# Reordering the head of a fused transformer block: the first scaled activations, tile 2's transposes, and a split last K tile used as cover

## The chip, the core and the metric

The kernel runs on one core of a Trainium2 chip. The metric is the device time of one execution in microseconds (us). TensorE does the matmuls ("PE" in the profile; "PEld" is its weight load), VectorE is "DVE", ScalarE "ACT", GpSimdE "POOL", and SyncE ("SP") issues most transfers (71 of 79 in the trace of before). Where a start time has three decimals, or a "stall" or "gap" is given in nanoseconds, it is worked out from the recorded starts of consecutive instructions: the distance from one matmul's start to the next, less what that shape usually takes.

## The reference

A diffusion transformer block on 2 x 256 tokens of width 1152, with six modulation vectors from `silu(c) @ w_mod`:

```python
mod = (_silu(c) @ w_mod).reshape(B, 6, 1, D)
shift_a, scale_a, gate_a, shift_m, scale_m, gate_m = [mod[:, i] for i in range(6)]
h = _layernorm(x) * (1 + scale_a) + shift_a
qkv = (h @ wqkv).reshape(B, N, 3, H, Dh)
# attention over 2 heads of 576, then
x = x + gate_a * (a @ wo)
h2 = _layernorm(x) * (1 + scale_m) + shift_m
return x + gate_m * (_gelu(h2 @ w_fc1) @ w_fc2)
```

Only the stretch up to the first Q matmul is changed. It needs LN1 of four token tiles (0 and 1 are batch 0, 2 and 3 batch 1), the scale sums, K = h @ wk from a "scaled h" without the shift (a shift of all keys by one vector leaves the softmax as it is), then the shift, and Q.

## The kernel before

Instructions stand in units; a list scheduler orders ACT and DVE, and PE keeps program order. The code hangs an increment of its engine's semaphore on each instruction that is not a transfer; the trace of before records 1754 of them on TensorE's, for 1755 matmuls:

```python
for ins in u.instrs:
    for (k, v) in waits[ins.gidx]:
        ...                                        # wait_ge on other engines' or transfers' semaphores
    bi = ins.fn(eng_handle)
    if ins.dma_sem is not None:
        bi.then_inc(dma_sems[ins.dma_sem], 16)
    else:
        bi.then_inc(sems[e], 1)
```

The head. `warm` issues dummy matmuls, `xn_T(t)` transposes a tile's normalised rows, `sca` is the first four column groups of the scale sums, `hk(kt, b)` scales one k-tile of one batch, `k_first(kt)` multiplies it into K for batch 0 (eight 256-column matmuls):

```python
xn_T(0); warm(1, "d"); sca(3, 6); warm(2, "e"); sca(6, 9)
hk(0, 0); sc1a(0, KC); hk(1, 0)
# ... (copies of tile 0/1's transposes, hk(2,0) and hk(3,0) on ACT)
xn_T(3, 0, 8)
xn_T(2, 0, 8)
k_first(0)
xn_T(3, 8, 9); xn_T(2, 8, 9)
k_first(1)
# ...
k_pair(range(KC), 0, 1); k_pair(range(KC), 1, 1)      # batch 1, first four k-tiles
sc_ones(KC, KT)
for kt in range(KT):
    mod_kt(WSC, kt, 0, "scb_%d" % kt, (KC, KT))        # 45 two-column matmuls: second scale sums
sc1a(KC, KT)                                           # copy 1 + scale out of PSUM
for kt in range(KC, KT):
    for b in range(2):
        hk(kt, b)                                      # scaled h of k-tiles 4..8
k_pair(range(KC), 2, 1)                                # eight matmuls, cover for sc1a and hk(4, 0)
# k-tiles 4..8 (the "fifth k-tile" is kt = 4) ...
k_pair(range(5), 3, 1, bank=1)
#   shift rows: 36 matmuls with two output rows, packed four column tiles wide
copy_on("dve", SHR[0:98, :], ...)                      # evict them
k_pair(range(5, KT), 3, 1, bank=1)                     # eight matmuls, cover for that
#   nine transposes of the shift rows, copied to SHA; h = scaled h + SHA
proj(WK, 8, 17, HK, 0)                                 # last K tile: nine 512-column matmuls, cover for that
```

The output stage, which the change doesn't touch, ends with stores of 96 and 64 columns whose matmuls (36 each) come last.

Of the kernel before, what the change touches and what calls it, by code (L numbers as in the profile page):

```python
# [500 lines left out]
P = 128  # L501
NTOK = 512
D = 1152
KT = 9
# [5 lines left out]
CH = 384  # L510
NCH = 3
F0 = 8
KC = 4
# [3 lines left out]
def c_mm(n):  # L517
    return max(n / 2.4 + 2.5, 27.0)
# [26 lines left out]
def build_kernel(nc, x, c, wqkv, wo, w_mod, w_fc1, w_fc2, out):  # L545
    S = Sched()
# [4 lines left out]
    with (  # L551
# [11 lines left out]
        def ps32(bank, c0=0, n=512):  # L563
            return psum[:, bank * 512 + c0: bank * 512 + c0 + n]
# [30 lines left out]
        WK = wmat(O_B, D)  # L595
        WO = wmat(O_B, D)
        WSH = wmat(O_C, D)
# [12 lines left out]
        HK = sb(O_HK, 9216).rearrange("p (k t) -> p k t", k=KT)  # L610
        QK = sb(O_QK, 18432).rearrange("p (j t) -> p j t", j=18)
# [19 lines left out]
        IDENT = sb(misc(256), 256)  # L631
# [4 lines left out]
        ST = sb(misc(36), 36)  # L636
        SHA = sb(misc(72), 72, F32)
        SC1A = sb(misc(72), 72, F32)
# [32 lines left out]
        def dma(dst, src, nbytes, name, is_out=False, eng="sp", run=4096):  # L671
            eff = 0.95 if run >= 4096 else (1.0 if run >= 2304 else (1.08 if run >= 1536 else 1.14))
            return S.op(eng, 500.0 if eng == "sp" else 150.0, lambda e: e.dma_start(dst, src), reads=[src], writes=[dst],  # L673
                        name=name, dma_bytes=nbytes * eff, is_out=is_out)
# [10 lines left out]
        def copy_on(eng, dst, src, n, psum16, name):  # L685
            if eng == "act":
                act(c_act(n), lambda e: e.activation(out=dst, in_=src, func=ACTF.Copy), [src], [dst], name)  # L687
            else:
                dve(c_dve_psum16(n) if psum16 else c_dve_psum32(n), lambda e: e.tensor_copy(dst, src), [src], [dst], name)  # L689

        def mm(o, l, r, st, sp, **kw):
            S.instr(lambda e: e.matmul(o, lhsT=l, rhs=r, start=st, stop=sp, **kw), reads=[l, r], writes=[o])  # L692
# [82 lines left out]
        def xn_T(t, ka=0, kb=KT):  # L775
            b = t // 2
            S.unit("pe", (kb - ka) * c_mm(128), "xnT_%d_%d" % (t, ka))
            for kt in range(ka, kb):
                tr(xslot(b, kt)[:, (t % 2) * 128:(t % 2) * 128 + 128], XN[:, t, kt * 128:(kt + 1) * 128], IDENT)
# [5 lines left out]
        def warm(n, tag, behind=None):  # L785
            for i in range(n):
                S.unit("pe", 300.0, "warm_%s_%d" % (tag, i))
                mm(ps32(2), IDENT, Q4B, True, True)
                if behind:
                    S.instrs[-1].deps.update(j for j in S.instrs[:-1] if j.name == behind)  # L790

        def mod_kt(W, kt, col0, name, fs=(0, 9)):
            S.unit("pe", (fs[1] - fs[0]) * 27.0, name)
            for f in range(*fs):
                mm(ps32(7, col0 + f * 2, 2), W[:, kt, f * 128:(f + 1) * 128], ST[:, kt:18:9], False, kt == KT - 1, skip_group_check=True)

        def sc1a(ka, kb):
            m, o = ps32(7, 2 * ka, 2 * (kb - ka)), SC1A[:, 2 * ka:2 * kb]
            dve(180, lambda e: e.tensor_copy(o, m), [m], [o], "sc1a_%d" % ka)


        def hk(kt, b, eng="dve"):
            dst = HK[:, kt, b * 256:(b + 1) * 256]
            s1 = ps32(7, 0, 1) if kt == 0 and b == 0 else SC1A[:, kt * 2 + b:kt * 2 + b + 1]
            src = xslot(b, kt) if kt < KC else HX[:, kt, b * 256:(b + 1) * 256]
            if eng == "act":
                act(c_act(256, 1), lambda e: e.activation(out=dst, in_=src, func=ACTF.Copy, scale=s1), [src, s1], [dst], "hk_%d_%d" % (kt, b))
                return
            dve(345 if kt < KC else 285, lambda e: e.tensor_scalar(out=dst, in0=src, scalar1=s1, scalar2=None, op0=ALU.mult),
                [src, s1], [dst], "hk_%d_%d" % (kt, b))  # L810
# [8 lines left out]
        ev_rr = [0]  # L819

        def k_pair(kts, i, b, bank=None):
            S.unit("pe", 2 * len(kts) * c_mm(256), "k%d_%d_%d" % (b, i, kts[0]))
            bank = KB[b][i] if bank is None else bank
            if kts[0] == 0:
                for kt in kts:
                    for half in range(2):
                        k_mm((kt,), 2 * i + half, b, bank, half)
            else:
                for half in range(2):
                    k_mm(kts, 2 * i + half, b, bank, half)  # L830
            if kts[-1] == KT - 1:
                eng = "act" if ev_rr[0] % 2 == 0 else "dve"
                ev_rr[0] += 1
                copy_on(eng, QK[:, 9 + 2 * i:11 + 2 * i, b * 256:(b + 1) * 256], ps32(bank).rearrange("p (j t) -> p j t", j=2), 512, False,
                        "k_ev%d_%d" % (b, i))
# [5 lines left out]
        def sc_ones(ka, kb):  # L841
            S.unit("pe", 60.0, "ones_%d" % ka)
            mm(ps32(7, 2 * ka, 2 * (kb - ka)), IDENT, ONES[:, 2 * ka:2 * kb], True, True)
# [8 lines left out]
        xn_T(0)  # L852
        warm(1, "d")
        sca(3, 6)
        warm(2, "e")
        sca(6, 9)
        hk(0, 0)
        sc1a(0, KC)
# [3 lines left out]
        hk(2, 0, "act")  # L862
        hk(3, 0, "act")
        xn_T(3, 0, 8)
        xn_T(2, 0, 8)

        def k_first(kt):
            for i in range(4):
                k_pair((kt,), i, 0)

        k_first(0)
        xn_T(3, 8, 9)
        xn_T(2, 8, 9)
        k_first(1)
        xn_T_copy(1, 4, 8, "act")
        xn_T_copy(1, 8, 9, "act")
        for kt in range(2, KC):
# [2 lines left out]
            hk(kt, 1)  # L880
        k_pair(range(KC), 0, 1)
        k_pair(range(KC), 1, 1)
        sc_ones(KC, KT)
        for kt in range(KT):
            mod_kt(WSC, kt, 0, "scb_%d" % kt, (KC, KT))
        sc1a(KC, KT)
        for kt in range(KC, KT):
            for b in range(2):
                hk(kt, b)
        k_pair(range(KC), 2, 1)  # L890
        for kt in range(KT):
            dma(WQ[:, kt, :], wqkv_v[:, kt, 0:D], P * D * 2, "ld_wq%d" % kt, run=2304)
# [7 lines left out]
                k_pair((KT - 2, KT - 1), i, b)  # L900

        def qk_evac(j, bank):
            copy_on("act" if ev_rr[0] % 2 == 0 or j in (6, 8) else "dve", QK[:, j, :], ps32(bank), 512, False, "qk_ev%d" % j)
            ev_rr[0] += 1

        def proj(W, j, dst_j, H, bank):
            S.unit("pe", KT * c_mm(512), "qk_%d" % dst_j)
            for kt in range(KT):
                mm(ps32(bank), W[:, kt, j * 128:(j + 1) * 128], H[:, kt, :], kt == 0, kt == KT - 1)
            qk_evac(dst_j, bank)  # L910

        sh_split = ((0, 3), (3, 5), (5, 7), (7, 9))
        SHR = sb(O_P, 768)
        k_pair(range(5), 3, 1, bank=1)
        S.unit("pe", KT * c_mm(CH) + 100.0, "shr")
        for kt in range(KT):
            for j, (f0, f1) in enumerate(sh_split):
                mm(psum[32 * j:32 * j + 2, 1024:1024 + (f1 - f0) * 128], ST[:, kt:18:9], WSH[:, kt, f0 * 128:f1 * 128],
                   kt == 0, kt == KT - 1, tile_position=(0, 32 * j))
        copy_on("dve", SHR[0:98, :], psum[0:98, 1024:1024 + CH], CH, False, "shr_ev")  # L920
        k_pair(range(5, KT), 3, 1, bank=1)
        S.unit("pe", KT * 27.0, "shT")
        for j, (f0, f1) in enumerate(sh_split):
            for f in range(f0, f1):
                mm(ps32(2, f * 2, 2), SHR[0:98, (f - f0) * 128:(f - f0 + 1) * 128], IDENT[0:98, 32 * j:32 * j + 2], f == 0, f == KT - 1,
                   skip_group_check=True)
        dma(WV, wqkv_v[:, :, 2 * D:3 * D], D * D * 2, "ld_wv", run=2304)
        for k0 in range(0, KT, 3):
            dma(WMODR[:, k0:k0 + 3, :], wmod_v[:, k0:k0 + 3, 2 * D:4 * D], 3 * P * 2 * D * 2, "ld_modr%d" % k0)
        MT1 = ps32(2, 0, 18)  # L930
        dve(170, lambda e: e.tensor_copy(SHA, MT1), [MT1], [SHA], "sha")
        for kt in range(KT):
            for b in range(2):
# [5 lines left out]
                else:  # L939
                    dve(260, lambda e, src=src, dst=dst, s2=s2: e.tensor_scalar(out=dst, in0=src, scalar1=s2, scalar2=None, op0=ALU.add),  # L940
                        [src, s2], [dst], "hx_%d_%d" % (kt, b))
        proj(WK, 8, 17, HK, 0)
        dma(WO, wo_v, D * D * 2, "ld_wo", run=2304)


        S.first = {
            "dve": ["zq4b", "c_half", "c_silu", "bn_ln1_1_0", "bn_ln1_1_1", "bn_ln1_1_2", "aggr_ln1_1", "veps_ln1_1", "bn_ln1_2_0",
                    "xn_1", "bn_ln1_2_1", "xn_0", "bn_ln1_2_2", "aggr_ln1_2", "var_ln1_3", "veps_ln1_2", "xn_3", "xn_2", "hk_0_0", "sc1a_0", "hk_1_0",
                    "hk_0_1", "hk_1_1", "hk_2_1", "hk_3_1", "sc1a_4"] + ["hk_%d_%d" % (kt, b) for kt in range(KC, KT) for b in range(2)],
            "act": ["ld_c", "c_tanh", "sum_ln1_0", "sq_ln1_0", "sum_ln1_3", "sq_ln1_3", "xnT_cp0_4", "xnT_cp0_8", "hk_2_0", "hk_3_0",  # L950
                    "xnT_cp1_4", "xnT_cp1_8"],
        }
# [293 lines left out]
        for t in range(4):  # L1246
            b = t // 2
# [88 lines left out]
```

## Time and profile before

| | |
|---|---|
| time | 245.73 us, median of 3 (245.61 to 245.73) |
| span of the profiled execution | 243.9 us |
| TensorE busy | 239.0 us, 98% |
| last matmul starts | 240.62 us |
| from there to the end of the program ("the tail") | 3.29 us |

The page of before: busy time of each engine with its share of the span and the number of instructions, and the chain that ended last by engine.

```profile
PE 239.0 (98%) x1755; PEld 147.4 (60%) x1755; DVE 120.9 (50%) x218; ACT 66.5 (27%) x134; POOL 21.3 (9%) x39
...
PE 91%; DMA 5%; SPq 2%; issue 0%; DVE 0%
```

The chain of before in order of time (start, us, what). Read from the end: TensorE alone from 18.73 us on, and before that one transfer of `w_mod`.

```profile
7.11 11.57 DMA arena<-in_w_mod_dram
18.68 0.05 issue
18.73 40.89 PE psum L692 x310
...
106.13 134.88 PE psum L692 x848
241.01 0.02 issue
241.03 0.24 DVE arena L1259
```

The timeline of before around that point (start, us, engine, line, operation; in brackets the idle time before and what ended it). TensorE waits for the last third of the second scale columns; by start times it loses 0.49 us. Then DVE's copy (L799) follows the last scale sum, which started at 19.107, after 0.31 us.

```profile
18.72 1.82 PEld L692 LDWEIGHTS psum<-arena 128*128 128x128 bf16 x29 [0.44 <-DMA arena<-in_w_mod_dram]
18.73 1.99 PE L692 MATMUL psum<-arena 128*128 128x2 bf16 x28 [0.35 <-DMA arena<-in_w_mod_dram]
19.42 0.17 DVE L799 COPY arena<-psum 128x10 f32<-128x10 f32 x1 [6.03 <-PE psum L692]
19.62 1.07 DVE L809 TENSOR_SCALAR arena<-arena 128x256 bf16<-128x256 bf16 x5
```

The head in the same timeline: normalisation of tiles 3 and 2 (L764, one after the other), first scaled h (L809), and K's first matmuls at 12.06.

```profile
10.32 1.23 DVE L764 TENSOR_SCALAR arena<-arena 128x1152 bf16<-128x1152 bf16 x2 [0.58 <-POOL arena L755]
11.13 1.09 PE L695 MATMUL psum<-arena 128*128 128x128 bf16 x16
11.46 0.35 DVE L809 TENSOR_SCALAR arena<-psum 128x256 bf16<-128x256 bf16 x1
12.06 1.04 PE L692 MATMUL psum<-arena 128*128 128x256 bf16 x8
```

These are the transfer queues of before between 240.4 and 243.6 us (packets, MB, share of 16 engines) and the last two output stores (size, us from issue to landing):

```profile
q1 hardware_dynamic: 288, 0.04, 7.8%
q8 instruction: 1, 0.02, 2.5%
...
out_dram<-arena SPq DMA_DIRECT2D x1, 24.0 KB, 2.6
out_dram<-arena SPq DMA_DIRECT2D x1, 16.0 KB, 1.8
```

### The profile page before, as it was taken

To read this page: it belongs to the slowest core of one execution; us is meant where nothing else is said; L and a number is where in the kernel's file an instruction comes from. 1 tells how busy PE (TensorE), PEld (TensorE's weight loads), DVE (VectorE), ACT (ScalarE), POOL (GpSimd) and SP (SyncE) were. 2 spreads that over 40 slices of the span, in tenths; PEclk is the share of its full clock that TensorE was granted. 3 is DMA by queue.
4 is the path that set the end of the run, shared out by engine and by line. 5 is a ranking of instruction groups with operands and counts; after the bars stand their busy time and mean duration, and the time that the engine had idled before them with its cause. 6 is when DMAs were issued, how large, how long until landed. Compare 5 with 4: busy or idle time off the path is not lost.

```text
span 243.9 us, 4070 instructions
## 1 busy us (share of the span) xinstructions
PE 239.0 (98%) x1755; PEld 147.4 (60%) x1755; DVE 120.9 (50%) x218; ACT 66.5 (27%) x134; POOL 21.3 (9%) x39
## 2 busy tenths in 40 slices
PE   7999999999999999999999999999999999999994
PEld 2698754556667666898444444444656565656584
DVE  3814398596997899689999500000022211111112
ACT  5730340345424206973233222223000000000000
POOL 1400000000021186400000000020000000000000
DMA  6999999999995999979953498030000000000000
GB/s 234 333 381 391 389 392 389 398 411 409 389 350 171 343 390 392 393 264 393 312 173 86 145 329 300 0 86 14 0 16 19 16 16 19 16 27 21 19 16 19
DMA packets 30140, 51.59 MB, mean 212 GB/s; under 512 B 1703, under 2 KB 15787, under 8 KB 30123
## 3 DMA queue, kind: packets, MB, share of 16 engines
q1 hardware_dynamic: 29680, 50.14, 57.5%
q0 software_dynamic: 416, 1.19, 1.6%
q8 instruction: 14, 0.23, 0.4%
q14 instruction: 3, 0.02, 0.0%
q10 hardware_dynamic: 27, 0.00, 0.0%
HBM read 50.14 MB, written 1.19 MB: 210 GB/s over the span
## 4 chain that ended last, share of the span: by engine, by line
PE 91%; DMA 5%; SPq 2%; issue 0%; DVE 0%
PE psum L692 90%; DMA arena<-in_w_mod_dram 5%; SPq L673 2%; PE psum L695 1%; DVE arena L1259 0%; DVE arena L1260 0%
## 5 line engine op out<-in xcount | busy, mean ns | idle before, releaser
L692 PE MATMUL psum<-arena 128*128 128x384 bf16 (+12 forms) x1666 | 235.8, 308 | 1.9 <-POOL arena L715 1.5
L692 PEld LDWEIGHTS psum<-arena 128*128 128x128 bf16 (+4 forms) x1666 | 142.2, 97 | 91.3 <-issue 4.7
L1054 DVE SCALAR_TENSOR_TENSOR arena<-arena 128x1152 f32<-128x1152 bf16 x32 | 44.7, 1413 | 0.6
L1259 DVE TENSOR_TENSOR arena<-psum,arena 128x384 f32<-128x384 f32 (+3 forms) x14 | 7.0, 500 | 68.0 <-PE psum L692 68.0
L1168 ACT ACTIVATE arena<-psum 128x512 bf16<-128x512 f32 (+1 forms) x44 | 22.4, 520 | 42.7 <-PE psum L692 42.7
L687 ACT ACTIVATE arena<-psum 128x512 bf16<-128x512 f32 (+6 forms) x35 | 19.0, 560 | 39.8 <-PE psum L692 39.1
L689 DVE CAST arena<-psum 128x512 bf16<-128x512 f32 (+3 forms) x14 | 8.9, 645 | 11.9 <-PE psum L692 11.9
L673 POOL DMA_DIRECT2D dit_scratch<-arena x3 | 1.8, 616 | 115.9 <-DVE arena L689 59.1
L1136 POOL TENSOR_TENSOR arena<-arena 128x384 f32<-128x384 f32 x12 | 10.9, 914 | 11.2 <-DVE arena L1135 9.6
L1081 DVE CAST arena<-psum 72x32 bf16<-72x32 f32 x1 | 0.2, 188 | 21.3 <-PE psum L692 21.3
L743 DVE BATCH_NORM_STATS2 arena<-arena 128x6 f32<-128x384 f32 (+1 forms) x18 | 9.5, 548 | 0.1
L1141 ACT ACTIVATE arena<-arena 128x1152 bf16<-128x1152 f32 x4 | 5.3, 1343 | 11.1 <-DVE arena L1140 11.1
L1135 DVE TENSOR_TENSOR arena<-psum,arena 128x384 f32<-128x384 f32 x12 | 6.5, 552 | 1.5 <-PE psum L692 1.4
L1260 DVE TENSOR_TENSOR arena<-arena 128x384 bf16<-128x384 f32 (+3 forms) x14 | 7.0, 501 | 0.5
L695 PE MATMUL psum<-arena 128*128 128x128 bf16 (+1 forms) x89 | 7.1, 219 | 0.0
L695 PEld LDWEIGHTS psum<-arena 128*128 128x128 bf16 (+1 forms) x89 | 5.8, 98 | 2.0 <-issue 0.8
L1158 ACT ACTIVATE arena<-psum,arena 128x128 bf16<-128x128 bf16 x16 | 6.0, 456 | 1.7 <-PE psum L695 1.1
L1155 DVE TENSOR_SCALAR arena<-psum,arena 128x128 bf16<-128x128 bf16 x20 | 5.4, 335 | 1.9 <-PE psum L695 1.9
L1061 DVE TENSOR_REDUCE arena<-arena 128x36 f32<-128x1152 f32 x4 | 5.4, 1346 | 0.0
L1058 DVE STREAM_TRANSPOSE arena<-arena 128x1152 f32<-128x1152 f32 x4 | 5.4, 1363 | 0.0
L984 ACT ACTIVATE arena<-psum,arena 128x256 bf16<-128x256 f32 x8 | 3.7, 472 | 1.3 <-PE psum L692 0.9
L980 DVE TENSOR_REDUCE arena<-psum 128x2 f32<-128x512 f32 x4 | 2.8, 689 | 1.8 <-PE psum L692 1.8
(47 smaller groups left out, 45.2 us busy)
## 6 DMA issues: line engine op xcount, KB each, us to landing
arena<-in_w_fc_dram SPq DMA_DIRECT2D x9, 1152.0 KB, 7.6
arena<-in_w_fc_dram SPq DMA_DIRECT2D x4, 2592.0 KB, 17.5
arena<-in_wqkv_dram SPq DMA_DIRECT2D x18, 288.0 KB, 10.2
arena<-in_w_mod_dram SPq DMA_DIRECT2D x3, 1728.0 KB, 20.2
arena<-in_w_mod_dram SPq DMA_DIRECT2D x3, 864.0 KB, 13.8
arena<-in_w_mod_dram SPq DMA_DIRECT2D x9, 288.0 KB, 10.5
arena<-in_wqkv_dram SPq DMA_DIRECT2D x1, 2592.0 KB, 16.6
arena<-in_wo_dram SPq DMA_DIRECT2D x1, 2592.0 KB, 24.4
```

The costliest lines, as they stand in the source:

```text
L673: return S.op(eng, 500.0 if eng == "sp" else 150.0, lambda e: e.dma_start(dst, src), reads=[src], writes=[dst], name=name, dma_bytes=nbyte ...
L687: act(c_act(n), lambda e: e.activation(out=dst, in_=src, func=ACTF.Copy), [src], [dst], name)
L689: dve(c_dve_psum16(n) if psum16 else c_dve_psum32(n), lambda e: e.tensor_copy(dst, src), [src], [dst], name)
L692: S.instr(lambda e: e.matmul(o, lhsT=l, rhs=r, start=st, stop=sp, **kw), reads=[l, r], writes=[o])
L695: S.instr(lambda e: e.transpose(o, i_, idn), reads=[i_, idn], writes=[o])
L743: dve(550, lambda e, s=s, o=o: e.bn_stats(out=o, in_=s), [s], [o], "bn_%s_%d" % (tag, ci))
L1054: dve(1270, lambda e, w=w, s=s, acc=acc: e.scalar_tensor_tensor(out=acc, in0=w, scalar=s, in1=acc, op0=ALU.mult, op1=ALU.add), [w, s, acc] ...
L1135: dve(550, lambda e, o=o, ga=ga, x1c=x1c: e.tensor_tensor(out=x1c, in0=o, in1=ga, op=ALU.mult), [o, ga], [x1c], "wo_t1_%d_%d" % (t, ci))
L1136: S.op("pool", 930, lambda e, xs=xs, x1c=x1c: e.tensor_tensor(out=x1c, in0=x1c, in1=xs, op=ALU.add), reads=[x1c, xs], writes=[x1c], name=" ...
L1168: act(c_act(ntok), lambda e: e.activation(out=dst, in_=o, func=ACTF.Gelu_apprx_tanh), [o], [dst], "gelu_%d_%d" % (f, tok0))
L1259: dve(c_dve_psum32(w), lambda e, o=o, gm=gm, t1=t1: e.tensor_tensor(out=t1, in0=o, in1=gm, op=ALU.mult), [o, gm], [t1], "fc2_t1_%d_%d" % ( ...
L1260: dve(c_dve_32(w), lambda e, t1=t1, x1c=x1c, ost=ost: e.tensor_tensor(out=ost, in0=t1, in1=x1c, op=ALU.add), [t1, x1c], [ost], "fc2_out_%d ...
```

## The change

The intent: let K start without waiting for tile 2, keep TensorE busy while the second scale columns arrive, and hide the shift rows' eviction. It does four things.

1. Head: DVE does the first scaled h before tile 2's normalisation, tile 2's transposes come behind the second k-tile, and one 512-column dummy goes.
2. The last K tile is split by batch into eighteen 256-column matmuls: four stand ahead of the second scale sums, seven between the shift rows and their transposes, seven behind (together with four matmuls of another K tile, moved there: eleven). The tile is copied out of PSUM in two halves instead of one.
3. The first scaled h of k-tile 4 is issued ahead of the copy `sc1a` and takes its scale straight from PSUM.
4. One K eviction goes from DVE to ACT.

```diff
-        warm(2, "e")
+        warm(1, "e")
...
-        xn_T(2, 0, 8)
...
         k_first(0)
+        k_first(1)
         xn_T(3, 8, 9)
-        xn_T(2, 8, 9)
-        k_first(1)
+        xn_T(2)
...
+        def k17(b, ka, kb):
+            for kt in range(ka, kb):
+                mm(ps32(7, 256 * (1 - b), 256), WK[:, kt, D - P:D], HK[:, kt, b * 256:(b + 1) * 256], b == 1 and kt == 0, kt == KT - 1,
+                   skip_group_check=True)
         sc_ones(KC, KT)
+        k17(0, 0, KC)
         for kt in range(KT):
             mod_kt(WSC, kt, 0, "scb_%d" % kt, (KC, KT))
+        hk(KC, 0)
         sc1a(KC, KT)
...
-        k_pair(range(5), 3, 1, bank=1)
+        k_pair(range(KT - 2), 3, 1, bank=1)
...                                              # shift rows, now into bank 0
-        k_pair(range(5, KT), 3, 1, bank=1)
+        k17(0, KC, KT)
+        k17(1, 0, 2)
...                                              # transposes of the shift rows
+        k_pair(range(KT - 2, KT), 3, 1, bank=1)
+        k17(1, 2, KT)
...
-        proj(WK, 8, 17, HK, 0)
...
-  "xn_3", "xn_2", "hk_0_0", "sc1a_0", "hk_1_0", "hk_0_1"        (order on DVE)
+  "xn_3", "hk_0_0", "sc1a_0", "hk_1_0", "xn_2", "hk_0_1"
```

The split tile shares PSUM bank 7 with the scale sums, with only one `start` flag of its own, on batch 1's first matmul. Batch 0's nine have none; in the code, the last one ahead of them in that bank is that of `sc_ones`, on the ten columns of the sums. What the flag does beyond those columns no trace shows.

More of the change, by code (lines that the diff above doesn't have):

```diff
@@ L803, in hk @@
             dst = HK[:, kt, b * 256:(b + 1) * 256]
-            s1 = ps32(7, 0, 1) if kt == 0 and b == 0 else SC1A[:, kt * 2 + b:kt * 2 + b + 1]
+            s1 = ps32(7, 2 * kt, 1) if kt in (0, KC) and b == 0 else SC1A[:, kt * 2 + b:kt * 2 + b + 1]
             src = xslot(b, kt) if kt < KC else HX[:, kt, b * 256:(b + 1) * 256]
@@ L831, in k_pair @@
             if kts[-1] == KT - 1:
-                eng = "act" if ev_rr[0] % 2 == 0 else "dve"
+                eng = "act" if ev_rr[0] % 2 == 0 or (i, b) == (3, 1) else "dve"
                 ev_rr[0] += 1
@@ L882, in build_kernel @@
         k_pair(range(KC), 1, 1)
+        def k17(b, ka, kb):
+            S.unit("pe", (kb - ka) * c_mm(256), "k17_%d_%d" % (b, ka))
+            for kt in range(ka, kb):
+                mm(ps32(7, 256 * (1 - b), 256), WK[:, kt, D - P:D], HK[:, kt, b * 256:(b + 1) * 256], b == 1 and kt == 0, kt == KT - 1,
+                   skip_group_check=True)
         sc_ones(KC, KT)
+        k17(0, 0, KC)
         for kt in range(KT):
             mod_kt(WSC, kt, 0, "scb_%d" % kt, (KC, KT))
+        hk(KC, 0)
         sc1a(KC, KT)
@@ L888, in build_kernel @@
             for b in range(2):
-                hk(kt, b)
+                if kt > KC or b:
+                    hk(kt, b)
         k_pair(range(KC), 2, 1)
@@ L902, in qk_evac @@
         def qk_evac(j, bank):
-            copy_on("act" if ev_rr[0] % 2 == 0 or j in (6, 8) else "dve", QK[:, j, :], ps32(bank), 512, False, "qk_ev%d" % j)
-            ev_rr[0] += 1
+            copy_on("dve" if j in (0, 2, 4) else "act", QK[:, j, :], ps32(bank), 512, False, "qk_ev%d" % j)
         def proj(W, j, dst_j, H, bank):
@@ L913, in build_kernel @@
         SHR = sb(O_P, 768)
-        k_pair(range(5), 3, 1, bank=1)
-        S.unit("pe", KT * c_mm(CH) + 100.0, "shr")
-        for kt in range(KT):
-            for j, (f0, f1) in enumerate(sh_split):
-                mm(psum[32 * j:32 * j + 2, 1024:1024 + (f1 - f0) * 128], ST[:, kt:18:9], WSH[:, kt, f0 * 128:f1 * 128],
-                   kt == 0, kt == KT - 1, tile_position=(0, 32 * j))
-        copy_on("dve", SHR[0:98, :], psum[0:98, 1024:1024 + CH], CH, False, "shr_ev")
-        k_pair(range(5, KT), 3, 1, bank=1)
+        k_pair(range(KT - 2), 3, 1, bank=1)
+        for k0 in range(0, KT, 3):
+            S.unit("pe", 3 * c_mm(CH) + 50.0, "shr_%d" % k0)
+            for kt in range(k0, k0 + 3):
+                for j, (f0, f1) in enumerate(sh_split):
+                    mm(psum[32 * j:32 * j + 2, 0:(f1 - f0) * 128], ST[:, kt:18:9], WSH[:, kt, f0 * 128:f1 * 128],
+                       kt == 0, kt == KT - 1, tile_position=(0, 32 * j))
+        copy_on("dve", SHR[0:98, :], psum[0:98, 0:CH], CH, False, "shr_ev")
+        k17(0, KC, KT)
+        k17(1, 0, 2)
         S.unit("pe", KT * 27.0, "shT")
@@ L924, in build_kernel @@
             for f in range(f0, f1):
-                mm(ps32(2, f * 2, 2), SHR[0:98, (f - f0) * 128:(f - f0 + 1) * 128], IDENT[0:98, 32 * j:32 * j + 2], f == 0, f == KT - 1,
+                mm(ps32(0, f * 2, 2), SHR[0:98, (f - f0) * 128:(f - f0 + 1) * 128], IDENT[0:98, 32 * j:32 * j + 2], f == 0, f == KT - 1,
                    skip_group_check=True)
+        k_pair(range(KT - 2, KT), 3, 1, bank=1)
+        k17(1, 2, KT)
+        for b in range(2):
+            copy_on("act", QK[:, 17, b * 256:(b + 1) * 256], ps32(7, 256 * (1 - b), 256), 256, False, "qk_ev17_%d" % b)
         dma(WV, wqkv_v[:, :, 2 * D:3 * D], D * D * 2, "ld_wv", run=2304)
@@ L929, in build_kernel @@
             dma(WMODR[:, k0:k0 + 3, :], wmod_v[:, k0:k0 + 3, 2 * D:4 * D], 3 * P * 2 * D * 2, "ld_modr%d" % k0)
-        MT1 = ps32(2, 0, 18)
+        MT1 = ps32(0, 0, 18)
         dve(170, lambda e: e.tensor_copy(SHA, MT1), [MT1], [SHA], "sha")
@@ L947, in build_kernel @@
             "dve": ["zq4b", "c_half", "c_silu", "bn_ln1_1_0", "bn_ln1_1_1", "bn_ln1_1_2", "aggr_ln1_1", "veps_ln1_1", "bn_ln1_2_0",
-                    "xn_1", "bn_ln1_2_1", "xn_0", "bn_ln1_2_2", "aggr_ln1_2", "var_ln1_3", "veps_ln1_2", "xn_3", "xn_2", "hk_0_0", "sc1a_0", "hk_1_0",
-                    "hk_0_1", "hk_1_1", "hk_2_1", "hk_3_1", "sc1a_4"] + ["hk_%d_%d" % (kt, b) for kt in range(KC, KT) for b in range(2)],
+                    "xn_1", "bn_ln1_2_1", "xn_0", "bn_ln1_2_2", "aggr_ln1_2", "var_ln1_3", "veps_ln1_2", "xn_3", "hk_0_0", "sc1a_0", "hk_1_0",
+                    "xn_2", "hk_0_1", "hk_1_1", "hk_2_1", "hk_3_1", "hk_%d_0" % KC, "sc1a_4", "hk_%d_1" % KC] + ["hk_%d_%d" % (kt, b) for kt in range(KC + 1, KT) for b in range(2)],
             "act": ["ld_c", "c_tanh", "sum_ln1_0", "sq_ln1_0", "sum_ln1_3", "sq_ln1_3", "xnT_cp0_4", "xnT_cp0_8", "hk_2_0", "hk_3_0",
```

## The prediction

> **What bounds the kernel now.** The page gives TensorE (PE) 239.0 of 243.9 us busy. In the chain of waits that ended last, PE has 91%, the w_mod DMA 5% and the DMA queue 2%. From 18.73 us the chain is PE alone, to 241.0 us. So only PE work after 18.73 us, and PE gaps there, are worth anything. Before it the chain is a transfer: the last piece of the second scale columns of w_mod, which PE awaits (timeline: idle 0.35 us before a matmul at 18.73, modelled ends; by start times 0.52 us where 0.03 is usual, so 0.49 us lost). The DMA engines are saturated there (share 1.0), so PE changes don't move that landing.
>
> The change feeds PE work into that hole. Around the shift rows, start times show only 0.09 us lost before and 0.10 us after the packed 2-row matmuls.
>
> **Unit costs, from start-to-start times.** 256-column matmul 109 ns, 512-column 215.7 ns, transpose 56 ns. [...] Vector end to PE start: about 0.06 us. Last matmul's start to dependent Vector start: about 0.31 us.
>
> **Head, before 18.73 us.** One 512-column dummy goes (-0.216). Vector's normalisation of tile 2 (10.97 us) no longer stands before the first scaled h, which moves from 11.46 to about 11.20 (estimate: the last sum matmul starts 0.216 earlier, at 10.885, plus 0.31), ready for PE at about 11.60. PE has then only tile 3's transposes to do, until about 11.40: a new stall of about 0.2 us. K's first k-tile starts 11.60 instead of 12.06, but ten transposes come after the second k-tile, so the third k-tile starts near 13.92, as before. Head gain: about zero, and DMA would hide it anyway.
>
> **The hole.** Four 256-column matmuls of the last K tile (0.437 us) go before the scale sums. PE reaches the last third of the sums at about 18.67; the data lands at about 18.68. Gap falls from 0.49 to about 0.05 us; resumption stays at 18.73.
>
> **After 18.73 us.** Before: nine 512-column matmuls, 1.941 us. After: fourteen of 256 columns, 1.529 us: -0.41 us. Splitting itself costs 18 x 109.2 - 9 x 215.7, about +0.025, included here. Seven matmuls (0.764 us) instead of eight cover the row eviction (0.558 us plus both latencies): estimated +0.05 us stall. The other eleven (1.20 us) cover shift copy and first shifted h, estimated to need about 1.0: no stall, also because the K eviction that delayed the shift copy on Vector (31.47 to 32.08) goes to Scalar. First Q matmul: 33.08 instead of 33.44. Later Q weights land over 1 us before use, so the shift carries to the end.
>
> **Prediction.** 245.73 - 0.36 = 245.37 us; 8 in 10 between 244.95 and 245.75. Faster by over 2%: 0.005; within 2%: 0.985; slower by over 2%: 0.01.
>
> **What shows it right.** The DMA wait near 18.7 nearly gone, PE's scale sums resuming at 18.7; a stall of about 0.2 us before K's first matmul near 11.6; Q starting near 33.1; unchanged PE stream afterwards. PE busy time falls little.
>
> **What would make it wrong.** The landing moves (another DMA order or run-to-run scatter) and the gain with it; the head stall is larger than 0.2, so PE arrives after the landing and each further 0.1 costs 0.1; shift copy or first shifted h late, stalling Q; the last K tile's shared PSUM bank adding waits at the scale readers; Scalar, given the K eviction, delaying a shifted h that Q needs.

-0.41 for the matmuls and +0.05 for the stall make -0.36 us. The unit costs are means of the trace of before, from start to start: 109.2 ns for 256 columns, 215.8 for 512, 55.8 for a transpose. There a weight load that waited for VectorE started 0.052 to 0.053 us after VectorE's end in three cases and 0.073 in a fourth, and TensorE lost 0.093 us ahead of the packed shift rows and 0.096 behind them. The nine Q weight tiles landed between 29.95 and 41.98 us, each at least 1.8 us before its first matmul. The DMA share from 18 to 20.5 us was 1.06; that TensorE's edits would therefore not move the landing, no run shows.

## The result, and the profile after

Measured: 245.2 us median of 4 (245.03 to 245.36), against 245.67 (245.38 to 245.73) for before. The ratio is 0.9983, 95% interval 0.9966 to 1.0. A ratio here is the mean time of one kernel's fast runs over the mean of the other's fast runs of the same rounds, so not quite the ratio of the medians. The predicted 245.37 lies 0.17 us off, inside the range. The traces show that it came about in another way than predicted.

```profile
PE 238.9 (98%) x1763; PEld 148.1 (61%) x1763; DVE 120.4 (49%) x217; ACT 67.2 (28%) x136; POOL 21.4 (9%) x39
...
PE 94%; ACT 2%; DMA 2%; DVE 1%; POOL 0%; issue 0%; DVEq 0%
```

The chain of after. The `w_mod` transfer is gone from it; it now leads back through tile 3's normalisation to the load of x.

```profile
0.80 3.96 DMA arena<-in_x_dram
...
10.69 0.59 DVE arena L764
11.28 0.05 issue
11.32 0.62 PE psum L695 x8
11.94 1.75 PE psum L692 x16
13.69 0.56 PE psum L695 x10
14.25 45.14 PE psum L692 x382
...
105.90 134.88 PE psum L692 x848
240.78 0.02 issue
240.80 0.24 DVE arena L1272
```

The final piece is 134.88 us long in both chains and starts 0.23 us earlier (105.90 against 106.13). So TensorE won 0.23 us, all of it before the shared stretch, and no more than that. The span fell by 0.61 (243.91 to 243.31). The other 0.38 came after the last matmul. The transfer queues of after in the same window, 240.4 to 243.6 us:

```profile
q1 hardware_dynamic: 297, 0.04, 8.7%
q14 instruction: 1, 0.01, 0.6%
...
out_dram<-arena SPq DMA_DIRECT2D x1, 24.0 KB, 2.1
out_dram<-arena SPq DMA_DIRECT2D x1, 16.0 KB, 1.4
```

The view counts packets that start in its window. No q8 packet starts in it: the last one began at 239.91 and was done at 240.97, before the final store was issued. Both stores land faster, 2.1 and 1.4 us instead of 2.6 and 1.8. (The q14 packet falls behind the stores.)

The scale sums and the head of after:

```profile
16.81 3.92 PE L692 MATMUL psum<-arena 128*128 128x256 bf16 x69
19.78 0.29 DVE L809 TENSOR_SCALAR arena<-arena,psum 128x256 bf16<-128x256 bf16 x1 [4.37 <-PE psum L692]
```

```profile
10.69 0.58 DVE L764 TENSOR_SCALAR arena<-arena 128x1152 bf16<-128x1152 bf16 x1 [0.60 <-POOL arena L755]
11.28 0.35 DVE L809 TENSOR_SCALAR arena<-psum 128x256 bf16<-128x256 bf16 x1
11.32 0.62 PE L695 MATMUL psum<-arena 128*128 128x128 bf16 x8 [0.17 <-DVE arena L764]
11.78 1.47 PE L692 MATMUL psum<-arena 128*128 128x256 bf16 x12
```

TensorE doesn't pause in the scale sums. But its last third starts at 18.84 rather than 18.73, and the transfer itself had landed at 17.68, a full microsecond earlier than in the trace of before. And DVE's first instruction that waits for the sums starts 0.565 us after the last of them (19.212), where before needed 0.312. Three theories came out of this.

- **Hole theory** (the prediction's): the scale transfer lands near 18.7 in every execution, and the four moved matmuls fill the time.
- **Straggler theory**: that landing scatters, so the hole is there only sometimes, and the gain must come from elsewhere.
- **Fetch theory**: part of the gain is the tail. The q8 packets (of the kind "instruction" in the profile, 16,384 bytes each) are taken for blocks of TensorE's instructions: there are 14 of them, and through the FC2 stretch they follow the matmuls (each a load and a matmul), in the trace of before 128, 128 and 129 apart and the last one 158, in that of after 128, 127, 134 and 145. That is an inference from the spacing. The last one lay on the final stores before (240.67 to 241.96 us), and since the changed kernel has eight matmuls more, its last one came earlier (239.91 to 240.97).

### The profile page after: what moved, and what is told of

Its sections match the earlier page's. It is cut to its first block, busy times and chain, and to the rows that moved or that the text cites. A ratio compares the mean times of both kernels' runs of the same rounds, so it can differ in the third digit from the quotient of the medians.

```text
span 243.3 us, 4087 instructions
## 1 busy us (share of the span) xinstructions
PE 238.9 (98%) x1763; PEld 148.1 (61%) x1763; DVE 120.4 (49%) x217; ACT 67.2 (28%) x136; POOL 21.4 (9%) x39
## 4 chain that ended last, share of the span: by engine, by line
PE 94%; ACT 2%; DMA 2%; DVE 1%; POOL 0%; issue 0%; DVEq 0%
PE psum L692 93%; PE psum L695 2%; DMA arena<-in_x_dram 2%; ACT arena L753 1%; ACT arena L751 1%; DVE arena L764 0%; POOL arena L755 0%; DVE arena L1272 0%; DVE arena L1273 0%; DVE arena L754 0%; DVE arena L746 0%; DVEq L476 0%
## 5 line engine op out<-in xcount | busy, mean ns | idle before, releaser
L692 PE MATMUL psum<-arena 128*128 128x384 bf16 (+10 forms) x1674 | 235.7, 307 | 1.5 <-POOL arena L715 1.5
L692 PEld LDWEIGHTS psum<-arena 128*128 128x128 bf16 (+3 forms) x1674 | 142.9, 97 | 90.1 <-issue 4.5
L687 ACT ACTIVATE arena<-psum 128x512 bf16<-128x512 f32 (+6 forms) x37 | 19.6, 550 | 38.7 <-PE psum L692 37.0
L689 DVE CAST arena<-psum 128x512 bf16<-128x512 f32 (+3 forms) x13 | 8.2, 641 | 11.4 <-PE psum L692 11.3
L951 ACT ACTIVATE arena<-arena 128x256 bf16<-128x256 bf16 x6 | 2.6, 498 | 3.9 <-DVE arena L945 3.9
```

The source lines that it names most:

```text
L687: act(c_act(n), lambda e: e.activation(out=dst, in_=src, func=ACTF.Copy), [src], [dst], name)
L689: dve(c_dve_psum16(n) if psum16 else c_dve_psum32(n), lambda e: e.tensor_copy(dst, src), [src], [dst], name)
L692: S.instr(lambda e: e.matmul(o, lhsT=l, rhs=r, start=st, stop=sp, **kw), reads=[l, r], writes=[o])
```

## The experiments

All outputs were correct. Times are medians; each kernel was timed against before.

### The two kernels again, and each half of the change alone

No edit in the first two. `head_only` is before with part 1 of the change; `tail_only` is the changed kernel with part 1 undone:

```diff
 head_only, against before                      tail_only, against after
-        warm(2, "e")                          -        warm(1, "e")
+        warm(1, "e")                          +        warm(2, "e")
     (and the order of xn_T, k_first and "xn_2" as in the diff above, or back)
```

> The kernel before once more, unchanged. Hole theory: the last third of the second scale columns lands at about 18.7 us in every execution, TensorE again loses about 0.5 us there. Straggler theory: the landing at 18.7 in the first trace was scatter; the same transfer landed at 17.7 in the trace of after, so here it lands at about 17.7 and TensorE loses nothing. Time ratio 1.000 within 0.001 either way; this is also the noise floor.

> The changed kernel once more. Hole theory: 0.36 to 0.5 us below before; no wait for the scale columns larger than 0.1 us. Straggler theory: under 0.15 us below before on average, since the four moved matmuls fill a hole that is there only now and then; head stall before tile 3's transposes near 0.2 to 0.3 us again.

> Before plus only the head part: first scaled h ahead of tile 2's normalisation, tile 2's transposes behind the second k-tile, one dummy fewer. Hole theory: no time change (within 0.1 us), the wait for the scale columns stays near 0.5 us or grows. Straggler theory: TensorE is not held by the transfer, so what the head saves (at most the dummy's 0.216 us, less a stall before tile 3's or K's first matmul) shows in the time: 0 to 0.2 us faster.

> The changed kernel with the head of before: the split last K tile as cover around the second scale sums and shift rows alone. Hole theory: all of the gain, 0.36 to 0.5 us below before. Straggler theory: no gain, 0.0 to 0.1 us slower than before (the split costs 0.025, the row eviction's shorter cover 0.05).

| | median (range), us | ratio to before (95%) |
|---|---|---|
| again_before | 246.08 (245.51 to 246.15) | 1.0008 (0.9995 to 1.0021) |
| again_after | 245.11 (245.04 to 245.50) | 0.9981 (0.9968 to 0.9995) |
| head_only | 245.73 (245.54 to 245.84) | 1.0000 (0.9987 to 1.0013) |
| tail_only | 245.34 (245.22 to 245.67) | 0.9986 (0.9973 to 0.9998) |

The times fit the hole theory: the head alone gives nothing, the rest gives most. The traces don't. The transfer landed at 18.68 in `again_before`, but TensorE lost only 0.083 us there, since it arrived late itself. In its place stood another stall, at 20.14, for the scaled h of the fifth k-tile. The timeline of `again_before`:

```profile
19.59 0.17 DVE L799 COPY arena<-psum 128x10 f32<-128x10 f32 x1 [5.79 <-PE psum L692]
19.80 0.87 DVE L809 TENSOR_SCALAR arena<-arena 128x256 bf16<-128x256 bf16 x4
20.14 0.44 PEld L692 LDWEIGHTS psum<-arena 128*128 128x128 bf16 x5 [0.25 <-DVE arena L809]
```

And in the profile of `tail_only` the last matmul started at 240.70, no earlier than before (240.62 and 240.77): the whole gain of that execution was the tail, 2.91 us instead of 3.2 to 3.3. The transfer landed at 19.12 there, so TensorE lost 0.41 us in spite of the cover; other executions may have lost less. So the hole theory got its expected time for `tail_only`, in the execution that was seen, from a cause that it doesn't contain.

### Moving the last instruction block alone

```diff
 before_f9, against before           after_f7, against after
-F0 = 8                             -F0 = 8
+F0 = 9                             +F0 = 7
```

F0 is the number of FC1 tiles that are computed in two 256-column halves. One more means nine more matmuls of the same arithmetic; two 256-column matmuls at 109.2 ns instead of one 512-column at 215.8 make 2.6 ns more for each of the nine.

> The kernel before with F0 = 9 instead of 8: one FC1 tile is computed as two 256-column halves instead of one 512-column piece. Same arithmetic, nine more matmuls late in the kernel, +0.02 us of TensorE time (9 x 2.6 ns). Fetch theory: the last 16 KB block of TensorE instructions is fetched about nine matmuls earlier, clear of the last output stores, so the time from the last matmul's start to the end of the program falls from 3.2-3.3 us to about 2.9, and the kernel is 0.3 to 0.4 us faster than before. Rival (the whole gain of the change comes from TensorE's stream): same time as before, tail 3.2-3.3 us.

> The changed kernel with F0 = 7: nine fewer matmuls late. Fetch theory: the last instruction block comes back onto the last stores, tail 3.2-3.3 us instead of 2.9, time only 0.1 to 0.25 us below before (0.3 above the changed kernel). Rival: same time as the changed kernel, 0.36 to 0.5 us below before. Risk: less cover between the second normalisation's transposes; a TensorE gap near 97 to 107 us would show it and would have to be taken off.

| | median (range), us | ratio to before (95%) | tail, us |
|---|---|---|---|
| before_f9 | 245.29 (245.21 to 245.48) | 0.9989 (0.9977 to 1.0001) | 2.91 |
| after_f7 | 245.34 (245.22 to 245.89) | 0.9994 (0.9982 to 1.0007) | 3.06 |

`before_f9` has none of the change's edits. Its last matmul started at 240.79, the latest of all profiled kernels, and yet its median is 0.40 us below that of before (245.69). The intervals reach 1, so the times alone wouldn't settle it. The transfer view does, window 240.4 to 243.6 us: no q8 packet starts in it, and the last store lands as fast as in the changed kernel. (The last fetch isn't gone: it ran from 240.27 to 241.52 and ended before the final store was issued, at 241.79.)

```profile
q1 hardware_dynamic: 301, 0.05, 8.8%
...
out_dram<-arena SPq DMA_DIRECT2D x1, 24.0 KB, 2.2
out_dram<-arena SPq DMA_DIRECT2D x1, 16.0 KB, 1.4
```

The reverse, `after_f7`, brought the packet back and slowed the stores:

```profile
q1 hardware_dynamic: 288, 0.04, 7.6%
q8 instruction: 1, 0.02, 1.8%
...
out_dram<-arena SPq DMA_DIRECT2D x1, 24.0 KB, 2.4
out_dram<-arena SPq DMA_DIRECT2D x1, 16.0 KB, 1.6
```

It gave back only half of the tail, less than expected; that fetch took 0.95 us where before's took 1.28, and so ended sooner. No TensorE gap arose near 97 to 107 us, so the risk did not come true.

### The order at the second scale copy

```diff
-        hk(KC, 0)
         sc1a(KC, KT)
+        hk(KC, 0)                 # scale read from the copy again, as in before
```

> The changed kernel with one part undone: the copy of the second scale sums goes first and the first scaled h of the second half reads its scale from that copy, as in before. Backlog theory: with no hole in the 45 two-column matmuls, their completion signals lag (0.565 us from the last one's start to Vector, against 0.31 after a hole), so this puts about 0.2 us of stall before K's fifth k-tile (near 20.1 us) and 0.2 us on the time. Rival (this reordering was not needed): no stall, no change.

Measured: 245.51 (244.79 to 245.72), ratio 0.9990 (0.9976 to 1.0004), so above the changed kernel's 0.9981 to 0.9983 by about what was expected, but within the noise. Its profile can't confirm the mechanism: in that execution the transfer landed at 19.15, TensorE lost 0.36 us at the sums in spite of the cover, and with this hole the delay to DVE was 0.310 again and no stall followed. That is a miss for the run, but it is one more point for the delay, and it shows that the cover doesn't always suffice.

### One more matmul of cover before the shift transposes

```diff
-        k17(1, 0, 2)
+        k17(1, 0, 3)
...
-        k17(1, 2, KT)
+        k17(1, 3, KT)
```

> The changed kernel with one more matmul of the last K tile ahead of the shift row transposes (eight instead of seven, ten instead of eleven behind). Expected: the 0.047 us stall before the shift transposes goes, no stall before Q (cover 1.09 us against about 1.0 needed); TensorE's last matmul 0.05 us earlier, also one run to beat both, though 0.05 us is within the noise of the times. Fetch position unchanged, tail 2.9 us.

Measured: 245.21 (245.02 to 245.41), ratio 0.9984 (0.9972 to 0.9996). The 47 ns stall at 31.78 us was gone, and there was none before Q. The last matmul started at 240.39, as in the changed kernel (240.39 and 240.40), because K's fifth tile had begun 0.04 to 0.05 us later. The edit works, and the times can't see it.

### The cover in the hole undone

```diff
         sc_ones(KC, KT)
-        k17(0, 0, KC)
...
-        k17(0, KC, KT)
+        k17(0, 0, KT)
```

> The changed kernel with only the cover in the hole undone: the four matmuls of the last K tile that stood ahead of the second scale sums stand after the shift rows instead (eleven matmuls there instead of seven). Same instruction count, so the tail after the last matmul stays 2.9 us. Hole theory: TensorE waits at the scale sums again (0.1 to 0.5 us, as far as the transfer's landing at 18.4 to 19.1 goes), fifth k-tile starts at about the same time as in the changed kernel (20.0 to 20.1), so the last matmul comes 0.25 to 0.4 us later (0.437 less the 0.047 stall that longer cover removes, less what the landing gave) and the kernel is only 0.0 to 0.2 us below before plus nothing else: ratio about 0.9995 to 0.999. Fetch-only theory (the gain is all in the tail): same time as the changed kernel, ratio 0.998.

> The kernel of no_cover once more, since its first profile caught the scale transfer landing early (18.2 us) and one of its six runs was off by 2.5 us. Hole theory: with a landing at the usual 18.5 to 18.7 TensorE, arriving at the last third of the sums at about 18.37, loses 0.15 to 0.35 us there, and the mean time is about 0.2 us above that of the changed kernel (245.2), so about 0.3 below before. If the cover is worth nothing on average: mean again 245.2, 0.45 to 0.5 below before. Tail 2.9 us in either case.

First call: 244.99, 245.15, 245.12, 247.69, 245.47, 245.27; ratio 1.0003 (0.9973 to 1.0034), which the single run at 247.69 (granted clock 0.993) spoils. Second: 245.14, 245.47, 246.06, 246.03, 245.21, 245.00; ratio 0.9989 (0.9953 to 1.0026), with a run of before at 314.54 (clock 0.758) left out, and one at 248.01 (clock 0.993) kept. In the two profiles the last matmul started at 240.36 and 240.37, at least as early as in the changed kernel, and TensorE did not wait at the sums at all: the transfer landed at 18.22 and 18.33, and TensorE came to it at 18.41 and 18.42. The timeline of `no_cover`, one unbroken piece of TensorE and DVE's first scaled h at 19.36:

```profile
16.82 3.93 PE L692 MATMUL psum<-arena 128*128 128x256 bf16 x69
19.36 0.29 DVE L809 TENSOR_SCALAR arena<-arena,psum 128x256 bf16<-128x256 bf16 x1 [3.94 <-PE psum L692]
```

So the hole theory's loss of 0.25 to 0.4 us didn't appear in either profile. Without the 247.69, the eleven runs have a mean of 245.36, against 245.21 for the changed kernel's nine (4 and 5 runs). That is 0.14 apart before rounding, with a standard error of about 0.13. What the cover is worth on average stays open; two runs near 246.05 could be late landings, but they weren't profiled. The landings allow an estimate. Without the cover TensorE comes to the last third at 18.41, with it at 18.84; each of the fourteen landings in the table below, plus the 0.046 us from landing to first matmul, then costs between 0 and 0.437 us less with the cover. In five of them that is nothing, and the mean is 0.17 us. This takes it that the edits don't move the landing, which no run shows.

### One completion signal per group of matmuls

```diff
-                    else:
+                    elif e != "pe" or ins is u.instrs[-1]:
                         bi.then_inc(sems[e], 1)
```

(The wait values are counted to match: every matmul of a unit has the unit's number.) `best` has this and the edit of `after_cover8`.

> The changed kernel with one semaphore increment per group of matmuls (on its last one) instead of one on every matmul; order and work unchanged. Backlog theory (completion signals of 45 two-column matmuls issued 26.6 ns apart queue up): the delay from the last scale sum's start to the first Vector instruction that waits for it falls from 0.565 us to about 0.31 even without a hole. Rival (the delay comes from the pipe or from Vector, not from the signals): 0.565 stays. On the time little is expected, 0.0 to 0.1 us below the changed kernel, since only 0.02 us is lost there.

> The changed kernel with both small edits: one increment per group of matmuls and eight instead of seven matmuls ahead of the shift row transposes. Meant to beat both: last matmul at 240.3 or a little earlier, tail 2.9 us, 0.4 to 0.6 us below before, 0.0 to 0.15 below the changed kernel, which the times may not resolve.

`one_signal`: 245.30 (244.79 to 245.48), ratio 0.9981 (0.9969 to 0.9993). The last scale sum started at 19.226 and DVE followed at 19.429:

```profile
19.43 0.29 DVE L814 TENSOR_SCALAR arena<-arena,psum 128x256 bf16<-128x256 bf16 x1 [4.00 <-PE psum L697]
```

That is 0.203 us, against 0.565 in the changed kernel with the same 45 matmuls and no hole. The expected 0.31 was too cautious: it contained a rest of the same queue. The time didn't change visibly. `best`: 244.93 (244.72 to 245.24), ratio 0.9972 (0.9960 to 0.9984). It is clearly below before. Against the changed kernel it is about 0.2 us lower, which these runs don't resolve. It was run at another time.

### All profiled executions side by side

From the traces, in us. "Landed" is the last third of the second scale columns; "lost at sums" is TensorE's gap there; "delay" runs from the last scale sum's start to the first DVE instruction that waits for it; "fetch end" is the end of the last q8 packet, counted, like the tail, from the last matmul's start.

| kernel | sums begin | landed | lost at sums | delay | stall at 5th k-tile | 5th k-tile starts | last matmul | fetch end | tail |
|---|---|---|---|---|---|---|---|---|---|
| before | 17.41 | 18.68 | 0.49 | 0.312 | 0 | 20.00 | 240.62 | 1.33 | 3.29 |
| again_before | 17.82 | 18.68 | 0.08 | 0.480 | 0.13 | 20.14 | 240.77 | 1.20 | 3.20 |
| head_only | 17.72 | 18.53 | 0.03 | 0.536 | 0.19 | 20.04 | 240.67 | 1.35 | 3.34 |
| before_f9 | 17.77 | 18.57 | 0.02 | 0.544 | 0.20 | 20.09 | 240.79 | 0.73 | 2.91 |
| tail_only* | 17.50 | 19.12 | 0.41 | 0.315 | 0 | 20.45 | 240.70 | 0.79 | 2.91 |
| after* | 17.58 | 17.68 | 0 | 0.565 | 0.02 | 20.13 | 240.39 | 0.57 | 2.91 |
| again_after* | 17.59 | 18.40 | 0 | 0.567 | 0.02 | 20.14 | 240.40 | 0.80 | 2.91 |
| after_f7* | 17.64 | 17.54 | 0 | 0.566 | 0.02 | 20.19 | 240.43 | 1.08 | 3.06 |
| after_sc1a_first* | 17.57 | 19.15 | 0.36 | 0.310 | 0 | 20.48 | 240.73 | 1.04 | 3.15 |
| after_cover8* | 17.63 | 18.65 | 0 | 0.565 | 0.02 | 20.18 | 240.39 | 0.54 | 2.91 |
| no_cover | 17.59 | 18.22 | 0 | 0.578 | 0.03 | 19.71 | 240.36 | 0.62 | 2.91 |
| no_cover_again | 17.60 | 18.33 | 0 | 0.577 | 0.03 | 19.72 | 240.37 | 1.00 | 2.96 |
| one_signal* | 17.60 | 18.58 | 0 | 0.203 | 0 | 20.12 | 240.33 | 0.89 | 3.06 |
| best* | 17.59 | 18.04 | 0 | 0.203 | 0 | 20.12 | 240.32 | 0.76 | 2.88 |

\* four matmuls of the last K tile (0.437 us) are already done when the fifth k-tile starts.

Three things can be read from it.

- **The tail.** It is 2.88 to 2.91 where the fetch ends within 0.80 us of the last matmul's start, and 2.96 to 3.34 from 0.89 on. The final store is issued 1.0 us after that start (0.82 in `one_signal` and `best`). Its issue took 332 to 336 ns in all kernels of the first group, and 336 to 716 ns in the second (716 in before). But the final store doesn't always set the end. In all fourteen profiles the program ended no sooner than 0.49 us after that store had landed, and no sooner than 0.89 us after the 24 KB store before it had; in `again_before`, `head_only`, `after_sc1a_first`, `one_signal` and `best` it was the 24 KB store that set the end. The position of the fetch follows the number of TensorE's matmuls. It began 0.42 and 0.13 us after the last matmul's start with 1754 of them (`head_only`, `after_f7`), 0.05 after it with 1755 (both of before), 0.25 to 0.48 ahead of it with 1763, and 0.32 and 0.52 ahead with 1764 (`tail_only`, `before_f9`).
- **The delay.** It depends on how many two-column matmuls ran without a pause: 15 after a hole of 0.36 us or more give 0.31, all 45 give 0.57, one signal per five gives 0.20. I read this as a queue of completion signals. An estimate from these: (0.565 - 0.203) / 45 = 8 ns of backlog for each matmul on top of the 26.6 ns from start to start, so about 35 ns for a signal; fifteen then make 0.203 + 15 x 0.008 = 0.32, and 0.31 was measured. The packed traces bear it out, since they also record the increments of TensorE's semaphore: in the twelve profiles with one signal per matmul the increments of these matmuls come 34.2 ns apart. In after, the last sum's increment came 0.541 us after its start, in `one_signal` 0.178, and DVE started 0.02 us behind the increment each time.
- **Hole and backlog are exchanged for each other.** In the four profiles with before's scale section (the first four rows), TensorE either waits for the data, or it doesn't and then waits for the delayed signal at the fifth k-tile. That tile starts at 20.00 to 20.14 in any case. With part 3 of the change the stall is 0.02 to 0.03 even with the full delay.

## Why the prediction was right or wrong

The time was right: 245.37 predicted, 245.2 and 245.11 measured. As an explanation it was right in part, and the closeness of the number owes something to luck: the tail, which it left out, gave about 0.3 us, and two of its reasons for the rest did not hold.

- **"Gap falls from 0.49 to about 0.05 us; resumption stays at 18.73": the step that failed.** It took one execution's landing for a fixed time, on the argument that transfers at a DMA share of 1.0 don't move, which one trace could not show. Over fourteen profiles the landing ran from 17.54 to 19.15. The 0.49 us were found in only one of the four profiles with before's scale section; the others lost 0.02 to 0.08 there. And `no_cover`, without the cover, reached the fifth k-tile at 19.71 and 19.72, the same as the changed kernel's 20.13 less the 0.437 of work moved ahead (19.69). In those executions the cover would have bought nothing. It is insurance: it lets TensorE arrive at 18.84 without loss, and it was too short for the landings of 19.12 and 19.15.
- **What took its place: in the first pair luck, in the second parts 1 and 3.** In the trace of after, the transfer landed at 17.68, before TensorE could have come to it even without the cover (18.41), so the 0.49 us of the first pair would have gone without it. In the second pair the sums began 0.24 us sooner, and 0.08 us at the sums and 0.11 at the fifth k-tile went as well. The prediction gave part 3 no worth. But when there is no hole, the signals are late, and before's order then stalls 0.13 to 0.20. "Head gain: about zero, and DMA would hide it anyway" was right for the head alone (`head_only`, 1.0000), and wrong as a judgement of its part in the whole: where the second half of x landed late (6.23 and 6.17 us), before began the sums at 17.82 and the changed kernel at 17.58. Where it landed early the new head costs time instead: in the first trace of before x had landed at 5.81 and the sums began at 17.41, while `after_sc1a_first`, with 5.79, began them at 17.57. With the old head the sums began between 17.41 and 17.82 over four profiles, with the new one between 17.57 and 17.72 over ten, so the new head mostly takes away the dependence on that landing. `head_only` spent its gain on the transfer and the backlog stall. So each of the two is worth little without the other. That they are what the TensorE part of the second pair comes from is read from the traces, not shown by an experiment; I had no run with just these two and before's last K tile.
- **"A new stall of about 0.2 us" before K: right, with its place depending on the input.** `again_after`, where x landed at 6.00, shows just that (0.193 us before K's first matmul). In the first trace of after, where x landed at 6.17, TensorE waited 0.30 us before tile 3's transposes instead.
- **Split and shift rows: right.** The stall before the shift transposes was predicted at 0.05 and was 0.047; no stall before Q; Q started at 33.22 rather than 33.08, late by what the fifth k-tile was late.
- **TensorE's total: -0.36 predicted.** The two pairs of profiles show -0.23 and -0.37 in the last matmul's start.
- **The tail was missing from the sum altogether.** "Unchanged PE stream afterwards" was taken to mean that nothing after it changes. The tail fell by 0.38 and 0.29 us in the two pairs, because the last instruction block was fetched ahead of the last stores and not on top of them. `before_f9` got it with none of the change's edits, 0.27 us by ratio (0.0011 x 245.7) and 0.40 by medians, and `after_f7` lost half of it. It is a side effect of the number of instructions.

In the two pairs the parts add up to 0.61 and 0.65 us, while the ratios give 0.42 to 0.47. The profiled executions of the changed kernel (245.03 and 245.04) are the fastest of its nine. So the split of the average gain between TensorE and tail is not settled, only that both are in it and that neither explains it alone.

Still open is what scatters the landing. In before, fifteen of that transfer's sixteen parts had landed by 17.34 and the last came at 18.68; an instruction block was being fetched from 15.40 to 16.51. The eleven landings from 18.22 to 19.15 go with fetches that began between 15.4 and 16.2, and the two earliest, 17.54 and 17.68, with fetches that began at 16.44 and 16.84 (`best`, with 16.77, had 18.04). That the fetch held up one of the sixteen would fit these times, but it is not shown: no run moved the fetch on purpose.

## What to carry to other kernels

One trace shows one execution: before filling a wait on a transfer, look at the same landing in several runs, and look for the next wait close behind it, which may take the gap's place at once (here 0.49 us in one execution, 0.08 and 0.13 in the next). Here 45 short matmuls that each signalled let their consumer start 0.565 us after the last one's start, and 0.203 with one signal per five; so try letting only the last one signal, or reading the result directly in the first consumer (the stall at the fifth k-tile was then 0.02 to 0.03 instead of 0.13 to 0.20). Below half a microsecond, look at the start of the last matmul and at the tail separately before crediting an edit: the number of instructions alone moved the end of this kernel by about 0.3 us.
